# The first network's blocks 5 to 8 in pairs by seven half-block products, with attention beside blocks 2 to 4

## The chip, the cores and the metric

The kernel runs on one core of a Trainium2 chip. The metric is device time in microseconds (us) of one execution; lower is better. A core has TensorE (PE, matrix products), VectorE (DVE), ScalarE (ACT), GpSimd (POOL) and SyncE (SP), which issues nearly all DMAs here. SBUF is the memory on the core, PSUM the eight banks that TensorE writes.

## The reference, cut to what matters

Chunked attention feeds two networks of two GEMMs each; all is float32.

```python
# q, k, v: (8, 8, 576, 64); every chunk of 64 positions attends to itself only
scores = matmul(q_c, k_c.T) / sqrt(64)
attn = exp(scores - max(scores));  attn /= sum(attn) + 1e-09
x = matmul(attn, v_c)             # as 4608 tokens x 512
# first network: w_in 512 x 2048, w_out 2048 x 512
h = x @ w_in;  x = maximum(0.01 * h, h) @ w_out
# second network, the same sizes, another activation
h = x @ w_in2
P = a[0] + a[1]*h + a[2]*h**2 + a[3]*h**3
Q = 1 + abs(b[0])*abs(h) + abs(b[1])*h**2
out = (P / (Q + 1e-06)) @ w_out2
```

## The kernel before

The 4608 tokens are nine blocks of 512. A hidden layer of 2048 is 16 slices `f` of 128. To keep float32's digits, every operand of a GEMM is split into a high half that TensorE takes whole and a low half (value minus high half), and three products are added for each tile: high by high, high by low, low by high (`PASSES`). So a slice of the first GEMM is 4 x 3 = 12 products of 128x512, and so is one of the second GEMM. ScalarE makes the high half by a copy, VectorE the low half by a subtraction.

The work comes in this order:

1. The start (`start_up`): attention of the first units of 128 tokens, the decoding of the first network's weights into SBUF, where all 16 slices stay, and blocks 0 and 1 of the first network, in an order from a small planner.
2. Blocks 2 to 7 of the first network, in a loop of steps. In step `s` TensorE does `gemm1` of one slice and `gemm2` of the slice two steps earlier; ScalarE applies the leaky rectifier (`act1a`, L569) and makes the high half (`act1b`, L576), VectorE the low half (`act1c`, L581). Every four steps, one attention unit of the next block is done beside it: scores (L460), maximum and difference (L468, L470), exponential (L477), sum and reciprocal (L482 to L484), scaling on GpSimd (L488), eight transposes of pieces on VectorE (`att_turn`, L496), product with the values (L532), high and low half of the result (L547, L545). `stage_w` decodes a piece of the second network's weights and writes it to DRAM, together with the sums of quarter matrices that step 5 needs.
3. Block 8's first GEMM, all 16 slices in a row (L971); the results wait in SBUF.
4. The second network's block 0, by itself: each of 16 steps has one slice of its first GEMM and one `task`, a slice of a second GEMM (here block 8's of the first network).
5. The second network's blocks 1 to 8 as four pairs. The first GEMM of two blocks by two slices is a 2x2 by 2x2 product of half matrices, done with seven products of six matmuls each (`product`, L1060) instead of eight, from sums of weights (`wa`) and of inputs (`xf_T`). There are 32 units of two slices; a unit holds the seven products and up to four `task`s. The copies, additions and the activation around it have written times within the unit; `UNIT` is 20.43. Four banks hold the results: `a` and `b` (one tile, `hab`), `c` and `d` (`hh`). ScalarE copies the first product to `b` and, after the second, to `c`; VectorE adds the third to `a` and `d`.

The order of instructions on every engine is that in which the program issues them (`tc.manual_schedule`). In step 5 that is the order of `events`, sorted by their written times; a written time does nothing but set this order. Waits between engines come from the tiles that instructions share.

Of the kernel before, what the change touches and what calls it, by code (L numbers as in the profile page):

```python
# [17 lines left out]
P = 128  # L18
# [15 lines left out]
NSTART = 2 * NF  # L34
L1, L2 = 2, 3
# [8 lines left out]
NPAIRS = 4  # L44
# [3 lines left out]

SHIFTS = {
# [166 lines left out]
def tile_kernel(ctx: ExitStack, tc: tile.TileContext, qt, kt, vt, w1, w2, a, b, out):  # L216
# [23 lines left out]
    def singles(pool, *names):  # L240
        return [pool.tile([P, 512], F32, name=nm) for nm in names]

    hh_ps = singles(ps_open("hhp"), "hh0", "hh1")
# [6 lines left out]
    def o_acc(dc, n):  # L250
        if not o_ps:
            ps_close("startp")
            o_ps.extend(singles(ps_open("accp"), "oa0", "oa1", "ob0", "ob1"))
        return o_ps[dc][:, :n]

    xd = [dram.tile([KC, P, n], F32, name=f"xd{i}") for i, n in enumerate(BLOCKS)]
    xf = [dram.tile([4, P, 2, TM], F32, name=f"xf{j}") for j in range(NPAIRS)]
# [10 lines left out]
    wd = dram.tile([NF, P, 2, 2, DM], F32, name="wd")  # L268
    ws = dram.tile([NF // 2, P, 4, 2, 256], F32, name="ws")
    raws = {}  # L270
# [8 lines left out]
    def load_raw(ph, n):  # L279
        f, a, b = piece(ph, n)  # L280
        nm = f"raw{ph}_{n}"
        src = (w1, w2)[ph][f][:, a * DM:b * DM].bitcast(U32)
        if ph == 0 and n < NEARLY:
            raw = wpool.tile([P, (b - a) * DM, 2], U32, tag=f"w{WIDE + n % 3}", name=nm)
        else:
            raw = rpool.tile([P, DM, 2], U32, tag="raw", name=nm, bufs=3)
        nc.sync.dma_start(out=raw.rearrange("p n w -> p (n w)"), in_=src)
        raws[ph, n] = raw
# [5 lines left out]
    def temps(ph, n):  # L294
        nm = f"{ph}_{n}"
        if ph == 0 and n < NEARLY:
# [5 lines left out]
            rpool.tile([P, DM], I32, tag="dm", name=f"dm{nm}", bufs=3),  # L302
# [46 lines left out]
    def decode_lo(ph, n):  # L349
# [5 lines left out]
        if ph == 1:  # L355
            for c, y in enumerate((hi, lo)):
                nc.sync.dma_start(out=wd[f][:, c, a, :], in_=y.bitcast(F32))
# [22 lines left out]
    def form_split(f, h):  # L380
# [6 lines left out]
        for c, y in enumerate((hi, lo)):  # L387
            nc.sync.dma_start(out=ws[f // 2][:, 2 * h:2 * h + 2, c, :], in_=y.bitcast(F32))

    def stage_ops():  # L390
        for k, (f, h, _) in enumerate(halves):
            if k == 0:
                load_raw(1, 0)
            if k + 1 < NH:
                load_raw(1, k + 1)
            decode_bits(1, k)
            decode_exp(1, k)
            yield
            decode_rest(1, k)
            decode_sign(1, k)  # L400
# [15 lines left out]
    def stage_w():  # L416
        next(staging, None)
# [15 lines left out]
    def load_qk(u):  # L433
        if u >= NU:
            return
        for nm, src in (("q", qt), ("k", kt)):
            ld[nm, u] = apool.tile([P, KC, P], F32, tag=nm, name=f"{nm}{u}")
# [6 lines left out]
    def load_v(u):  # L444
        if u >= NU:
            return
        ld["v", u] = apool.tile([P, 512], F32, tag="v", name=f"v{u}")
# [16 lines left out]
    def att_max(u, ps):  # L464
        s = ps[:, :, 0:256].rearrange("p j (h t) -> p j h t", h=KC)
        mx = apool.tile([P, 8], F32, tag="mx", name=f"mx{u}")
        e = e0[u % 2] if u < NTURN else apool.tile([P, 8, CH], F32, tag="e", name=f"e{u}", bufs=1)
        V.tensor_reduce(out=mx.rearrange("p (j h) -> p j h", j=2), in_=s, axis=AX.X, op=ALU.max)  # L468
        att["e", u] = e
# [8 lines left out]

    def att_norm(u):
        e = att["e", u]  # L480
        sm = att["s", u] = apool.tile([P, 8], F32, tag="sm", name=f"sm{u}")
        V.tensor_reduce(out=sm, in_=e, axis=AX.X, op=ALU.add)  # L482
# [54 lines left out]
    def att_out(u, ps, x, off, lo):  # L537
# [8 lines left out]
        else:  # L546
            nc.scalar.activation(out=xh, in_=pv, func=AF.Copy)  # L547

# [71 lines left out]
    def finish(ph, i, share=False, cut=False):  # L620
        n = BLOCKS[i]
        for dc in range(KC):
# [8 lines left out]
            if ph == 0 and 0 < i < NB - 2 and (i % 2 or dc > 1):  # L631
                later.append((i, dc))

    later, held = [], []

    def split_later():
        if held:
            split_out(*held.pop())

    def reload_later():  # L640
        if later:
            i, dc = later.pop(0)
            held.append((i, dc, reload(i, dc)))
# [9 lines left out]
    def reload(i, dc):  # L653
        y = ypool.tile([P, TM], F32, tag="y", name=f"yr{i}_{dc}")
        nc.sync.dma_start(out=y, in_=xd[i][dc])
        return y

    x2 = {}

    def load_x2(i):  # L660
        x = new_x(1, i)
        for kc in range(KC):
            x2[kc] = ypool.tile([P, TM], F32, tag="y", name=f"x2_{i}_{kc}")[:, :BLOCKS[i]]
            nc.sync.dma_start(out=x2[kc], in_=xd[i][kc])

    def split_x2(i, kc):
        y, x = x2.pop(kc), xt[1, i]
        nc.scalar.activation(out=x[:, 0, kc, :], in_=y, func=AF.Copy)
        nc.vector.tensor_tensor(out=x[:, 1, kc, :], in0=y, in1=x[:, 0, kc, :].bitcast(F32), op=ALU.subtract)
# [13 lines left out]


    def start_up():
# [48 lines left out]
        def fin(s):  # L734
# [6 lines left out]
            "qk": load_qk, "v": load_v, "S": lambda u: att_scores(u, at_bk(u)), "mx": lambda u: att_max(u, at_bk(u)),  # L741
# [10 lines left out]
        for key, n in ordered(start_ops()):  # L752
            run[key](n)

    TAGX = [f"w{k}" for k in (0, 1, 2, 3, 4, 5, 6, 11, 15)]
    TAGB, TAGA, TAGO = ("w7", "w10"), ("w8", "w12"), ("w9", "w13", "w14")
    FORMS = ("B11", "T2", "T3", "T4", "B21", "T1", "B22")
    BASE = {"B11": 0, "B21": 1, "B22": 2}
    SUMS = {"T1": 0, "T2": 1, "T3": 2, "T4": 3}
    HALF = NF // 2  # L760
    NU2 = NPAIRS * HALF

    def second(npool, at_new):
        S, G = nc.scalar, nc.gpsimd
# [4 lines left out]
        def blocks_of(j):  # L769
            return 1 + 2 * j, 2 + 2 * j  # L770

        def sums_load(j, q, t):
            kc, c = q // 2, slice(q % 2 * 256, q % 2 * 256 + 256)
            i0, i1 = blocks_of(j)
            for x, (i, k) in enumerate(((i0, kc), (i1, kc), (i0, kc + 2), (i1, kc + 2))):
                nc.sync.dma_start(out=t[:, x], in_=xd[i][k][:, c])

        FORMED = ((3, 3, 1, "subtract"), (1, 1, 0, "subtract"), (0, 3, 0, "add"), (2, 2, 0, "subtract"))

        def sums_make(j, q, t, eng, step):  # L780
            kc, c = q // 2, slice(q % 2 * 256, q % 2 * 256 + 256)
            x, a, b, op = FORMED[step]
            eng.tensor_tensor(out=t[:, x], in0=t[:, a], in1=t[:, b], op=getattr(ALU, op))
            if step == 3:
                for x, nm in ((1, "T1"), (0, "T2"), (3, "T3"), (2, "T4")):
                    nc.sync.dma_start(out=xf[j][SUMS[nm]][:, kc, c], in_=t[:, x])

        xform = {}

        def x_load(j, n):  # L790
            nm, q = FORMS[n], len(FORMS) * j + n
            t = wpool.tile([P, 2, 2, TM], F32R, tag=TAGX[q % len(TAGX)], name=f"xf{j}_{nm}")
            xform[j, nm] = t
            if nm in SUMS:
                nc.sync.dma_start(out=t[:, 1].bitcast(F32), in_=xf[j][SUMS[nm]])
            else:
                nc.sync.dma_start(out=t.bitcast(F32), in_=xs[j][BASE[nm]])

        def x_hi(j, n):
            t = xform[j, FORMS[n]]  # L800
            S.activation(out=t[:, 0], in_=t[:, 1].bitcast(F32), func=AF.Copy)

        def x_lo(j, n, eng=V):
            t = xform[j, FORMS[n]]
# [563 lines left out]
```

## Time and profile before

| | |
|---|---|
| median of 3 runs | 1622.99 us (1622.93 to 1623.69) |
| profiled execution, whole | 1622.95 us |
| its span, first to last instruction | 1620.7 us |
| PE busy | 1603.5 us, 99% |
| DVE busy | 1211.5 us, 75% |
| ACT busy | 908.8 us, 56% |
| POOL busy | 264.3 us, 16% |
| moved by DMA | 309.85 MB, mean 191 GB/s |

Busy times are from one profiled execution. Products are pipelined and their ends are modelled: six in a row show 1.52 us where the next six begin 1.36 us later, and a wait inside a group of products shows as a longer group, not as idle time. PE's share is thus an upper limit of what it really does.

### The profile page before, as it was taken

What the parts mean: (1) busy time and instruction counts of PE and PEld (TensorE: products, weight loads), DVE (VectorE), ACT (ScalarE), POOL (GpSimd) and SP (SyncE); (2) the same over time, 40 slices, a digit from 0 to 9 for tenths busy, and PEclk for the clock granted to TensorE, in tenths of its full rate; (3) what the DMA queues carried; (4) which work ended last, traced back from release to release, by engine and by line L of the source; (5) the groups of instructions that cost most, each with busy time, mean ns of one, the idle gap of its engine ahead of it and who ended that gap; (6) DMA issues with size and microseconds to landing.
All of it is one profiled execution on the core that took longest, in us unless ns stands there. A gap on an engine that the chain in (4) does not pass through costs nothing.

```text
span 1620.7 us, 24054 instructions
## 1 busy us (share of the span) xinstructions
PE 1603.5 (99%) x9199; PEld 1317.1 (81%) x9199; DVE 1211.5 (75%) x1665; ACT 908.8 (56%) x1292; POOL 264.3 (16%) x163
## 2 busy tenths in 40 slices
PE   8999999999999999999999999999999999999998
PEld 7888788888878888888887778788888888888877
DVE  7986567666575766665257789899999999998972
ACT  7754233333433334343267777787778777777751
POOL 0000000000000000000012234333433343322210
PEclk9999999999999999999999999999999999999999
DMA  8621236343544346262466478777887778765545
GB/s 293 220 99 66 60 127 192 124 140 128 188 141 147 124 150 188 93 195 66 161 223 214 147 243 271 258 283 262 301 293 286 240 264 275 285 221 193 178 133 178
DMA packets 152401, 309.85 MB, mean 191 GB/s; under 512 B 13536, under 2 KB 46560, under 8 KB 145504
## 3 DMA queue, kind: packets, MB, share of 16 engines
q1 hardware_dynamic: 151856, 307.68, 56.8%
q8 instruction: 72, 1.18, 0.3%
q10 hardware_dynamic: 432, 0.66, 0.1%
q14 instruction: 41, 0.34, 0.1%
HBM read 242.22 MB, written 66.06 MB: 190 GB/s over the span
## 4 chain that ended last, share of the span: by engine, by line
PE 87%; DVE 6%; ACT 4%; issue 1%; DMA 1%; SPq 0%; ACTq 0%; DVEq 0%
PE hh L560 24%; PE oa L594 11%; PE ob L594 10%; PE ob L903 10%; PE oa L903 10%; PE hab L1063 10%; PE hh L1063 7%; PE hab L903 1%; PE hh L903 1%; PE at L460 1%; PE at L532 1%; ACT us L941 1%; DVE us L963 1%; DVE us L960 1%; DVE u L960 1%
## 5 line engine op out<-in xcount | busy, mean ns | idle before, releaser
L560 PE MATMUL hh<-x,w 128*128 128x512 f32 x1920 | 459.9, 390 | 0.1
L560 PEld LDWEIGHTS hh<-x,w 128*128 128x128 f32 x1920 | 359.9, 188 | 75.3 <-DVE x L545 0.5
L569 ACT ACTIVATE t<-hh 128x512 f32<-128x512 f32 x128 | 76.4, 597 | 286.2 <-PE hh L560 268.2
L947 POOL TENSOR_TENSOR u<-u,ah 128x1024 f32<-128x1024 f32 x64 | 154.3, 2413 | 275.1 <-ACT u L1102 262.0
L594 PE MATMUL oa<-g,w 128*128 128x512 f32 x768 | 198.8, 394 | 0.0
L594 PE MATMUL ob<-g,w 128*128 128x512 f32 x768 | 194.8, 389 | 0.0
L581 DVE TENSOR_TENSOR g<-t,g 128x512 fp32r<-128x512 f32 x128 | 90.5, 707 | 123.9 <-ACT g L576 119.5
L903 PE MATMUL oa<-gh,wo 128*128 128x512 f32 x512 | 178.8, 389 | 0.1
L903 PE MATMUL ob<-gh,wo 128*128 128x512 f32 x512 | 178.4, 389 | 0.0
L594 PEld LDWEIGHTS ob<-g,w 128*128 128x128 f32 x768 | 144.2, 188 | 30.2
L594 PEld LDWEIGHTS oa<-g,w 128*128 128x128 f32 x768 | 141.9, 188 | 30.2
L488 POOL TENSOR_TENSOR e<-e,sm 128x512 f32<-128x512 f32 x23 | 25.6, 1113 | 710.5 <-DVE sm L484 640.6
L903 PEld LDWEIGHTS oa<-gh,wo 128*128 128x128 f32 x512 | 96.1, 188 | 20.4 <-DVE y L923 0.5
L903 PEld LDWEIGHTS ob<-gh,wo 128*128 128x128 f32 x512 | 96.1, 188 | 20.1
L903 PE MATMUL oa<-gl,wo 128*128 128x512 f32 x256 | 99.9, 390 | 0.6 <-DVE gl L887 0.6
L1063 PE MATMUL hab<-xf_B,wb 128*128 128x512 f32 x384 | 97.7, 390 | 2.3 <-DVE gn L953 1.2
L496 DVE STREAM_TRANSPOSE pt<-e 32x256 f32<-32x256 f32 x224 | 97.5, 435 | 3.2
L903 PE MATMUL ob<-gl,wo 128*128 128x512 f32 x256 | 99.6, 389 | 0.0
L1063 PE MATMUL hh<-xf_T,wa 128*128 128x512 f32 x384 | 97.4, 389 | 0.0
L960 DVE SCALAR_TENSOR_TENSOR u<-u,ah 128x1024 f32<-128x1024 f32 x64 | 78.2, 1222 | 23.5 <-ACT ah L1113 23.4
L1063 PEld LDWEIGHTS hab<-xf_B,wb 128*128 128x128 f32 x384 | 71.8, 188 | 18.3 <-DVE sb L953 1.7
L576 ACT ACTIVATE g<-t 128x512 fp32r<-128x512 f32 x128 | 80.6, 630 | 6.7 <-PE ob L594 3.8
(194 smaller groups left out, 2652.1 us busy)
## 6 DMA issues: line engine op xcount, KB each, us to landing
wo<-wd SPq DMA_DIRECT2D x144, 512.0 KB, 5.6
wa<-ws SPq DMA_DIRECT2D x32, 1024.0 KB, 7.7
raw<-in_w SPq DMA_DIRECT2D x46, 512.0 KB, 5.1
wb<-wd SPq DMA_DIRECT2D x32, 512.0 KB, 4.4
xf_B<-xs SPq DMA_DIRECT2D x12, 1024.0 KB, 6.8
q<-in_q SPq DMA_DIRECT2D x36, 256.0 KB, 4.0
raw<-in_w SPq DMA_DIRECT2D x9, 1024.0 KB, 4.9
v<-in_v SPq DMA_DIRECT2D x36, 256.0 KB, 4.2
```

The source lines that it names most:

```text
L460: nc.tensor.matmul(ps[t, j, hp * CH:hp * CH + CH], q[r, hp, t], k[r, hp, t], start=True, stop=True)
L488: eng.tensor_tensor(out=e, in0=e, in1=sm.rearrange("p (h o) -> p h o", o=1).to_broadcast([P, 8, CH]), op=ALU.mult)
L496: nc.vector.transpose(pt[c + b:c + b + 32, :, a:a + 32], e[c + a:c + a + 32, :, b:b + 32])
L560: nc.tensor.matmul(ps, w[wp][:, 0, kc * P:(kc + 1) * P], x[:, xp, kc, :], start=(kc == 0 and (wp, xp) == (0, 0)), stop=(kc == KC - 1 and ( ...
L569: nc.scalar.activation(out=t, in_=ps, func=AF.Prelu, alpha=0.01)
L576: nc.scalar.activation(out=gh, in_=t, func=AF.Copy)
L581: nc.vector.tensor_tensor(out=gl, in0=t, in1=gh.bitcast(F32), op=ALU.subtract)
L594: nc.tensor.matmul(o_acc(dc, n), w[wp][:, 1, dc * P:(dc + 1) * P], g[gp], start=(first and (wp, gp) == (0, 0)), stop=(last and (wp, gp) == ...
L903: nc.tensor.matmul(acc(ph, i, dc), w[:, wp, c] if ph else wt[0, f][wp][:, 1, c], g[gp], start=(f == 0 and (wp, gp) == (0, 0)), stop=(f == ...
L947: G.tensor_tensor(out=u, in0=u, in1=ah, op=ALU.mult)
L960: V.scalar_tensor_tensor(out=u, in0=u, scalar=C1, in1=l, op0=ALU.add, op1=ALU.mult)
L1063: nc.tensor.matmul(bank, wform[:, wp, kc * P:kc * P + P], x[:, xp, kc, :], start=start and kc == 0 and (wp, xp) == PASSES[0], stop=kc == 1 ...
```

## The change

Three stages take the place of stages 2 and 3, and stages 4 and 5 are fed from them.

- `alone`: blocks 2 to 4 of the first network, 48 steps of a slice as before. All 23 attention units that the start leaves are done beside them, one every 10.95 of written time (a step has 5.45). Those of blocks 5 to 8 go to DRAM in one piece per unit (`att_store`, `xa`). A unit's exponential is taken head by head on ScalarE straight from PSUM, with the negated maximum as bias and the sum as a second output (`att_heads`), so that VectorE's difference and sum fall away. q, k and v have one buffer each. GpSimd joins both halves of the first network's weights again and forms their sums (`keep_w`, `first_sums`); they go to DRAM, as the second network's do. `stage_w` decodes 12 of 32 half slices here.
- `first_pairs`: blocks 5 to 8 as two pairs, 16 units of two slices, by the seven products. The units of the first pair have two `task`s each, those of the second four. Weights and inputs come from DRAM as one piece and are split on the core (`w_hi`, `w_lo`, `x_hi`, `x_lo`). An input form lies in SBUF as four runs of 128 columns for each half (`by_unit`). The activation is one Prelu. `stage_w` decodes the other 20 half slices, six or nine steps a unit.
- The second network's block 0: as before one slice and one `task` a step (two in the first two), now with written times too, and with splits of second weights and of the first pair's inputs between.

Every call of these stages and of the second network's pairs has a written time, to which a table `MOVED` of 840 entries adds its own, and `run_events` issues them sorted. The weights' DRAM copies are laid out anew so that a unit's are one DMA each. The start's list of operations, the second network's scheme of 32 units and the end stay.

```diff
@@ constants
-NPAIRS = 4
+NPAIRS, NPAIRS1 = 4, 2
+ALONE = range(2, len(BLOCKS) - 2 * NPAIRS1)
+CUT = 12
+STEP = 5.45
+MOVED = {
+    "t.act1b.11": -1.4, "t.act1b.21": 4.0, "t.act1b.25": 1.2, "t.act1b.26": 4.6, "t.act1b.33": 3.5, "t.act1b.41": 1.6,
...
@@ attention
+def att_heads(u, ps, half):
...
+    for h in range(4 * half, 4 * half + 4):
+        j, hp = divmod(h, KC)
+        nc.scalar.activation(
+            out=e[:, h], in_=ps[:, j, hp * CH:hp * CH + CH], func=AF.Exp, scale=1.0 / math.sqrt(D),
+            bias=mx[:, h:h + 1], accum_out=sm[:, h:h + 1],
+        )
+def att_store(u, ps):
...
+    nc.scalar.activation(out=y.rearrange("p h (c t) -> p c h t", c=2), in_=pv, func=AF.Copy)
+    nc.sync.dma_start(out=xa[u // 4][u % 4], in_=y.rearrange("p h t -> p (h t)"))
@@ the first network's weights
+def keep_w(f):
...
+    nc.gpsimd.tensor_tensor(out=v, in0=w[:, 0, 1, :], in1=w[:, 1, 1, :], op=ALU.add)
+    nc.sync.dma_start(out=wod[0][f // 2][:, f % 2], in_=v)
+def first_sums(k, step):
+    G = nc.gpsimd
...
+            G.tensor_tensor(out=v[-1], in0=w[:, 0, 0, :], in1=w[:, 1, 0, :], op=ALU.add)
...
+    G.tensor_tensor(out=s[:, 0], in0=a21, in1=a22, op=ALU.add)
+    G.tensor_tensor(out=s[:, 2], in0=a11, in1=a21, op=ALU.subtract)
+    G.tensor_tensor(out=s[:, 1], in0=s[:, 0], in1=a11, op=ALU.subtract)
+    G.tensor_tensor(out=s[:, 3], in0=a12, in1=s[:, 1], op=ALU.subtract)
+    nc.sync.dma_start(out=ws[0][k], in_=s)
@@ events
+def at(t, fn, *args):
+    key = f"{part_now[0]}.{fn.__name__.replace('<lambda>', 'f')}"
+    n = named[key] = named.get(key, -1) + 1
+    count[0] += 1
+    t += MOVED.get(f"{key}.{n}", 0) + 1e-6 * count[0]
+    events.append((t, len(events), fn, args))
@@ products
+def product(wform, x, bank, start, by_unit):
+    if by_unit:
+        x = x.rearrange("p c k (u t) -> p c (k u) t", u=2)
+    for kc in range(2):
+        for wp, xp in PASSES:
+            nc.tensor.matmul(
+                bank, wform[:, wp, kc * P:kc * P + P], x[:, xp, :, kc * P:kc * P + P] if by_unit else x[:, xp, kc, :],
...
+def attend(m):
+    n, t = UNITS[m], AT0 + EVERY * m
+    into_x = n // 4 < ALONE.stop
+    at(t, lambda: att_scores(n, at2))
+    if m + 1 < len(UNITS):
+        at(t + 0.8, load_qk, UNITS[m + 1])
...
+    at(t + 4.3, att_scale, n)
+    for x in range(8):
+        at(t + 5.6 + 0.9 * x, att_turn, n, x // 4, (x % 4,))
+    at(t + 15.0, lambda: att_values(n, at2))
@@ first_pairs, one unit
+        P11, PS2, PS3, P22, P12, PS1, PS4 = PT = (
+            (0.0, 2.72, 1.36, 6.8, 8.16, 9.52, 13.6), (0.0, 4.09, 8.17, 9.53, 10.9, 12.26, 16.34)
+        )[full]
+        for x in ((4.08, 10.88), (1.36, 5.45, 13.62, 17.7))[full]:
+            at(t + x, task)
...
+        at(t + P11 + 1.45, copy, b, a)
+        at(t + PS2 + 1.42, copy, c, a)
+        at(t + PS3 + 1.4, keep)
+        at(t + P12 + 1.4, add, a, a)
+        at(t + PS1 + 1.4, add, d, c)
+        at(t + P12 + 2.2, leaky, 0)
+        at(t + PS1 + 2.2, leaky, 1, 1)
+        at(t + PS4 + 1.4, leaky, 1, 0)
...
+        t += UNIT if full else 14.96
@@ the second network's block 0, one step
+        todo = [(one_block, s)] + [(one_act, s, x) for x in range(5)]
...
+            if s and x == 0:
+                todo += [(finish_one, s - 1, y) for y in range(3)]
+            todo.append((task,))
...
+        for n, call in enumerate(todo):
+            at(STEP * (s - NF + n / len(todo)), *call)
```

## Rows read from the trace of the kernel before

**Rows 1.** The page: busy time, share of the span and instructions of each engine.

```profile
PE 1603.5 (99%) x9199; PEld 1317.1 (81%) x9199; DVE 1211.5 (75%) x1665; ACT 908.8 (56%) x1292; POOL 264.3 (16%) x163
```

**Rows 2.** TensorE's waits: who for whom, us in total, times, longest.

```profile
PE hab L1063 <- DVE sb L953: 1.1, 1, 1.1
...
PE at L532 <- DVE pt L496: 1.1, 1, 1.1
...
PE hab L1063 <- ACT hab L1176: 0.7, 1, 0.7
```

**Rows 3.** Stretches: their length, busy time of each engine, granted clock, DMA share, GB/s.

```profile
200.00:300.00 100.00, 100.00 (x706) 82.00 (x703) 69.41 (x138) 35.74 (x61) 4.59 (x4) 1.00 0.47 148
...
822.00:866.00 44.00, 43.87 (x192) 35.50 (x192) 30.64 (x43) 30.25 (x47) 9.23 (x8) 1.00 0.59 207
...
913.00:1076.00 163.00, 159.26 (x694) 129.14 (x693) 144.10 (x139) 125.87 (x150) 59.76 (x35) 1.00 0.76 259
1076.00:1240.00 164.00, 164.00 (x725) 135.79 (x724) 152.84 (x139) 126.13 (x149) 59.44 (x34) 1.00 0.83 284
```

**Rows 4.** Timeline of TensorE, start and length: the start, and block 8's products.

```profile
10.55 1.06 PE L504 MATMUL hh<-ident,ep 128*128 128x128 f32 x8
...
783.06 40.96 PE L560 MATMUL hh<-x,w 128*128 128x512 f32 x180
```

**Rows 5.** The chain that ended last, block 2: start, length, what.

```profile
221.27 1.59 PE oa L594 x6
...
244.35 1.59 PE oa L594 x6
```

**Rows 6.** The same chain, in the second network's block 0.

```profile
847.59 0.82 ACT us L941
...
849.10 0.70 DVE sa L950
...
850.49 0.44 DVE g L855
...
851.09 0.70 DVE us L960
...
853.39 0.82 ACT us L941
```

**Rows 7.** Timeline of VectorE and GpSimd in the second network's pairs.

```profile
1088.14 2.39 POOL L947 TENSOR_TENSOR u<-u,ah 128x1024 f32<-128x1024 f32 x1 [0.85 <-ACT u L1102]
1088.39 3.23 DVE L887 TENSOR_TENSOR gl<-sb,gh 128x1024 fp32r<-128x1024 f32 x1
...
1102.45 1.22 DVE L887 TENSOR_TENSOR gl<-sb,gh 128x1024 fp32r<-128x1024 f32 x1
...
1105.61 2.41 POOL L947 TENSOR_TENSOR u<-u,ah 128x1024 f32<-128x1024 f32 x1 [15.08 <-ACT u L1102]
1106.23 0.68 DVE L950 TENSOR_TENSOR sb<-sb,hh 128x512 f32<-128x512 f32 x1
```

**Rows 8.** Groups of instructions by line: count, busy us, mean ns of one, idle before.

```profile
L496 DVE STREAM_TRANSPOSE pt<-e 32x256 f32<-32x256 f32 x224 | 97.5, 435 | 3.2
...
L581 DVE TENSOR_TENSOR g<-t,g 128x512 fp32r<-128x512 f32 x128 | 90.5, 707 | 123.9 <-ACT g L576 119.5 <-PE oa L594 3.7
...
L569 ACT ACTIVATE t<-hh 128x512 f32<-128x512 f32 x128 | 76.4, 597 | 286.2 <-PE hh L560 268.2 <-DVE g L581 8.2 <-DVE raw L378 7.3
...
L1183 DVE TENSOR_TENSOR hab<-hab,p 128x512 f32<-128x512 f32 x32 | 22.2, 695 | 6.2 <-PE hab L1063 6.2
...
L947 POOL TENSOR_TENSOR us<-us,tmp 128x512 f32<-128x512 f32 x16 | 20.8, 1299 | 155.4 <-ACT us L941 155.4
...
L547 ACT ACTIVATE x<-at 128x512 fp32r<-128x512 f32 x33 | 19.7, 598 | 58.1 <-DVE e L470 55.3 <-PE at L522 1.5 <-PE at L460 1.2
...
L699 ACT ACTIVATE ep<-ep,sm 128x64 f32<-128x64 f32 x64 | 16.1, 335 | 1.9 <-DVE sm L484 1.9
...
L805 DVE TENSOR_TENSOR xf_T<-xf_T 128x1024 fp32r<-128x1024 f32 x10 | 12.1, 1214 | 0.0
```

More of the change, by code (lines that the diff above doesn't have):

```diff
@@ L490, in att_scale, with att_turn @@
         )
-    def att_turn(u, half):
+    def att_turn(u, half, parts=range(4)):
         e, c = att["e", u], half * CH
-        for n in range(4):
+        for n in parts:
             a, b = n // 2 * 32, n % 2 * 32
@@ new lines, in tile_kernel @@
+    tasks, ready = [(0, ALONE[-1], NF - 2), (0, ALONE[-1], NF - 1)], {}
+    for j in range(NPAIRS1):
+        for i in blocks_of(0, j):
+            tasks.extend((0, i, f) for f in range(NF))
+    N1 = len(tasks)
+    for f in range(NF):
+        tasks.append((1, 0, f))
+    for j in range(NPAIRS):
+        for i in blocks_of(1, j):
+            tasks.extend((1, i, f) for f in range(NF))
+    late = len(tasks) - NF
+    tasks[late - 2:late + 4] = tasks[late:late + 4] + tasks[late - 2:late]
+    halved, done = [2], [0]
@@ new lines, in split_lo1, with task @@
+    def split_lo1(n):
+        t = tasks[n]
+        g, sub = ready.pop(t)
+        gh, gl = gt[t]
+        V.tensor_tensor(out=gl, in0=g, in1=gh.bitcast(F32), op=ALU.subtract)
+        left_of[sub] -= 1
+        if not left_of[sub] and sub in make:
+            free.append(sub)
+    def task(last=False):
+        ph, i, f = t = tasks[done[0]]
+        n = done[0]
+        done[0] += 1
+        g = gt.pop(t)[:2]
+        q = n // 2
+        for dc in range(KC):
+            for wp, gp in PASSES:
+                c = slice(dc * P, dc * P + P)
+                nc.tensor.matmul(
+                    acc(ph, i, dc), wo[q][:, wp, n % 2, c] if q else wt[0, f][wp][:, 1, c], g[gp],
+                    start=(f == 0 and (wp, gp) == (0, 0)), stop=(f == NF - 1 and (wp, gp) == PASSES[-1]),
+                )
+            if last:
+                put_last(dc)
+        if n % 2:
+            load_o(q + 3)
@@ new lines, in multiply, with copy @@
+    def multiply(ph, u, wname, nm, bank, start):
+        if wname[0] == "S":
+            w = wa[ph, u][:, :, int(wname[1]) - 1]
+        else:
+            c = {"A11": 0, "A12": 256, "A22": 512}[wname]
+            w = wb[ph, u][:, :, c:c + 256]
+        product(w, xform[ph, u // HALF, nm], bank, start, not ph)
+    def copy(to, of):
+        S.activation(out=to, in_=of, func=AF.Copy)
+    back = {}
+    UNITS = [13, 14, 15, *range(20, 25), *range(16, 20), *range(25, 36)]
+    UNITS = [n for n in UNITS if n < 4 * NB]
@@ L1051, in second @@
-        sb = xpool.tile([P, 4, 2, TM], F32, tag="x", name="sb")
-        for k in range(4):
-            make["sb", k] = lambda k=k: sb[:, k]
-            free.append(("sb", k))
-        make["n", 2] = lambda: ntile(2, "gn2")
-        free.append(("n", 2))
-        live = {}
-        ab, (d, c) = at_new, hh_ps[:2]
-        def product(wform, x, bank, start):
-            for kc in range(2):
+        for sub in (("w", 0), ("w", 1)):
+            if sub in free:
+                free.remove(sub)
+            del make[sub]
@@ new lines, in second, with finish_one, pre @@
+        for k in range(3):
+            make["n", k] = lambda k=k: ntile(k, f"gn{k}")
+            free.append(("n", k))
+        tmp, us = ntile(8, "tmp"), ntile(9, "us")
+        chain = {}
+        S.activation(out=warm, in_=cst[:, 0:1], func=AF.Abs_reciprocal_sqrt)
+        def finish_one(s, step):
+            u, t = chain[s]
+            (act_l, act_r, act_g)[step](*(u, tmp[:, 1], t)[:3 if step == 2 else 2])
+        def pre(n):
+            split_hi1()
+            split_lo1(n)
+        plan = {s: [(x_load, 1, 0, s)] for s in range(6)}
```

893 lines of the change are left out of this document (514 added, 379 removed), and 162 rows, old and new, of the table MOVED.

## The prediction

> **What bounds the kernel now.** I began with the page's busy row: TensorE is busy 1603.5 of 1620.7 us [rows 1]. The profiled execution took 1622.95 us, 2.25 more than its span and within 0.05 of the median of the runs, so the sum below is made against 1622.95. Next came the table of waits [rows 2]: TensorE's named waits are single events of about a microsecond. The stretches [rows 3] then say where the other engines stand. While the first network runs VectorE has 69 of 100 us; in the pairs of the second network it has 152.8 of 164 and the DMA engines 0.83, and yet TensorE is never idle there. So VectorE at 93% and 284 GB/s can be carried by this kernel without a loss, and what TensorE no longer has to do comes off the end, wherever the other engines keep up. The granted clock is 1.00 in every stretch, so the price of a product is one number: 180 in a row took 40.96 us, of which the last one's modelled tail is 0.16, so 0.2267 us each and 2.72 us for twelve [rows 4].
>
> Two places hide time that the idle column doesn't show. One attention unit costs TensorE 1.32 us: four steps with one unit are 244.35 - 221.27 = 23.08 us, and four steps alone are 4 x 5.44 = 21.76 [rows 5]. And where the second network's first block runs alone, a step takes 853.39 - 847.59 = 5.80 us instead of 5.44 [rows 6]: one round goes ScalarE 1.51, first products on VectorE, the split of the next half (850.49 to 851.09, 0.60), three more on VectorE, back to ScalarE, which writes a buffer that the last of them still read. About ten steps ran at this pace: some 3.7 us lost while PE counts as busy.
>
> **The change, part by part.** *Products.* Four blocks of the first network took 4 x 16 x 12 = 768 products in their first GEMM. Two pairs by seven half-block products take 2 x 8 x 7 x 6 = 672. The 96 that go are 96 x 0.2267 = 21.76 us; one dummy product more gives 0.23 back. The second GEMM, attention and the start keep their counts. A pair's unit with two tasks is (42 + 24) x 0.2267 = 14.96 us, one with four 20.40.
>
> The moving operand of the new products is read in four runs of 128 elements with gaps (`by_unit`). No product of the kernel before does so. Below, the cost is nothing: ScalarE reads four such runs in 598 ns and one of 512 in 597 [rows 8]. Above, each run costs like a product of 128 columns: eight took 1.06 us [rows 4], so 4 x 0.133 - 0.227 = 0.30 us times 672, or 204 us. I take nothing, since the ScalarE row is the same access pattern and the upper row also loads weights each time.
>
> *Attention beside blocks 2 to 4.* Its 23 units x 1.32 us of TensorE are moved, not removed; a unit now comes every two steps, 12.2 us. The stage is 48 x 5.44 + 23 x 1.32 = 292 us. VectorE's share of it: 48 low halves at 0.71 make 34, 184 turns at 0.435 make 80 [rows 8], maxima, sums and outputs some 37 (an estimate, 0.7 for each 512), twelve staged halves at about 5.1 (six instructions of 512 and a quarter of the sums, each 0.7 as an estimate from L581) 61, eleven low halves of 1024 at 1.21 13, so 225 of 292, 77%. ScalarE's eight exponentials by head cost 8 x 0.335 = 2.7 us a unit against one of 0.6 now: 48 us more in 292 where it has 36 in 100 [rows 3, 8], and the low half isn't needed for some two steps, so I price them at nothing. If that cover went, 2.1 us a unit would be 48 us. q, k and v keep one buffer each: the next unit's load waits at the head of SP's queue for the scores, and staging's loads and stores behind it; it is due 0.8 us after the scores and then has 11 us to land, so nothing for this either.
>
> GpSimd gets new work here: 32 additions of 512 at 1.30 [rows 8], 48 of 256 at half of that and the 23 scalings at the same 1.30, some 103 us. At 1088.39 a VectorE subtraction with two SBUF inputs took 3.23 us, having begun 0.25 us into a GpSimd multiplication of 2.39; the same one takes 1.22 with GpSimd idle [rows 7]. So an overlap costs VectorE up to the rest of the GpSimd instruction, 0.5 us on average here. GpSimd works in 35% of the stage, and some 150 VectorE instructions have two SBUF inputs: 150 x 0.35 x 0.5 = 26 us, which makes 251 of 292, still 86%. What is queued behind is the low half, two steps early, and the turns, for which the values product waits; such a wait happened once before, 1.1 us [rows 2]. I take 1 us for the stage; its bounds are 0 and 23 x 0.5 = 11.
> The Trainium skill (SBUF — State Buffer, "Who interferes with whom") says that a VectorE instruction with two SBUF inputs and a GpSimd instruction that reads SBUF exclude each other for the whole instruction. The 3.23 us agree; taken to its end, this rule is the second rival below.
>
> *The pairs.* Bank use follows the second network's scheme. The tight place is the copy of the first product's bank: ScalarE has one 1.36 us product in which to do a 0.58 us copy, and where ScalarE was late there before, TensorE waited 0.7 [rows 2]. Eight short units make 0 to 5 us. VectorE per short unit: two additions 1.4, two splits 1.4, three low halves of 1024 3.5, staging at most 5.3, so 11.6 of 14.96; per long unit at most 17.5 of 20.4. ScalarE has about 10.2 of 14.96. All are under the 93% and 77% that cost nothing [rows 3]. A short unit moves 0.52 (second weights), 0.79 and 0.52 (first weights and sums), 1.37 (staging), 0.46 (inputs), 0.65 MB (sums, outputs): 4.3 MB or 288 GB/s, just above the 284 of [rows 3]. I take 2 us for the pairs; bounds 0 and 16.
>
> *The second network's first block.* Its 16 steps and 18 tasks are 34 x 2.72 = 92.5 us. On VectorE stand 16 x 3.6, 18 splits at 0.69, twelve low halves of 1024 at 1.21 (six are new, of the second GEMM's weights, and two more of inputs), copies 2.8, one double split 1.9: 89 us, 96%. In its favour the split is written ahead of the round or behind it in many steps, which takes 0.60 off the 5.80. Against it, an addition of 1.21 fits the 1.51 us in which VectorE waits for ScalarE, but not together with the split: 5.20 + 1.21 + 0.69 - 1.51 = 5.59 in twelve steps is 1.8 us lost, and 6.4 where it fits nowhere is 11.7. I take 4, against 3.7 now: +0.3.
>
> *Entry to the second network's pairs.* The window shows 163 - 159.26 = 3.7 us idle [rows 3], partly waits for sums and banks [rows 2] that follow a burst of splits and additions; the sums are now made well before and the first product is issued early, but low halves are pushed into these units. I take 2: -1.7. The end is unchanged.
>
> Sum: 1622.95 - 21.76 + 0.23 + 1 + 2 + 0.3 - 1.7 = **1603 us**.
>
> **Rivals.**
> 1. *The pairs are bound by transfers or banks.* For it: 288 GB/s is the most this kernel would have carried for so long, and each low half stands behind a load. Against: 284 left TensorE no idle time. At the 259 GB/s of the window before it [rows 3] a short unit takes 16.6 us: 8 x 1.64 = 13 us, or 1603 - 2 + 13 = 1614. 12%.
> 2. *GpSimd holds VectorE in the attention stage; slower.* If all 103 us of GpSimd hold it, VectorE needs 225 + 103 = 328 us in a stage of 292: +36, 1603 - 1 + 36 = 1638. It decides from about 86 us held (292 - 225 + 19). For it, [rows 7]; against, half of VectorE's instructions there have one SBUF input, and one with a PSUM input took 0.68 beside GpSimd's 2.41. Half as much gives waits for turns, 1610. 12%, of which 3% for slower.
> 3. *The gaps slow the products.* Slower from 21.5 / 672 = 32 ns each. 3%.
> 4. *Better than the sum.* The first block's loss and the entry's go entirely: 1603 - 6 - 3 = 1594. 11%.
> My forecast, 1597 to 1608, has the rest, 62%.
>
> **Numbers.** The range takes in the forecast, the milder part of the second rival and about half of the first and the fourth, some 8 in 10: 1595 to 1613. Two runs of this kernel differ by 0.05%, so 0.2% (3.2 us) is about what can be told from no change. Slower than that: 3 + 3 = 6%; within it, 2%, from the tails of the first two rivals; faster, 92%.
>
> **What would show it.** 96 fewer products and 1580 to 1585 us of busy PE; new products at 1.36 us per six (rival 3: more); units of 14.96 and 20.4 us; in the attention stage 12.2 us per two steps, and values that don't wait for turns (rival 2: VectorE subtractions over 1 us, and waits for `pt`); no waits for loads in the pairs (rival 1); steps of 5.44 to 5.6 in the first block. I'd be wrong if the gaps cost time, or if a late low half stops TensorE once per unit.

## The result, and the profile after

The new kernel takes **1606.78 us** in the median of five runs (1606.05 to 1609.44). Its ratio to the kernel before is **0.9902 [0.9887, 0.9916]**, so it is about 16 us faster; 1603 had been forecast, within 1595 to 1613. The profiled execution below is the slowest of the five, 1609.44 us; a second profile comes with `new_again`.

The page's busy row, which answers to [rows 1]:

```profile
PE 1589.9 (99%) x9104; PEld 1302.0 (81%) x9104; DVE 1297.7 (81%) x1709; ACT 1018.7 (63%) x1714; POOL 400.0 (25%) x277
```

There are 95 products fewer: 96 went, the dummy came. VectorE has 86 us more work, ScalarE 110, GpSimd 136. The stretches, as in [rows 3]: the attention stage (first three), the first network's pairs (next two), the second network's first block, the entry to its pairs.

```profile
200.00:300.00 100.00, 97.75 (x796) 77.26 (x789) 74.72 (x140) 41.03 (x141) 38.21 (x33) 0.98 0.55 186
300.00:400.00 100.00, 97.68 (x880) 77.32 (x869) 78.17 (x144) 48.39 (x177) 52.74 (x49) 1.00 0.67 226
400.00:525.00 125.00, 125.00 (x1118) 98.98 (x1117) 93.81 (x193) 69.97 (x222) 22.50 (x22) 1.00 0.65 216
525.00:645.00 120.00, 120.00 (x531) 99.34 (x531) 85.72 (x121) 70.77 (x106) 18.89 (x20) 1.00 0.91 302
645.00:810.00 165.00, 164.21 (x725) 135.60 (x724) 123.81 (x181) 98.83 (x151) 17.82 (x14) 1.00 0.87 291
810.00:905.00 95.00, 95.00 (x420) 78.41 (x419) 84.44 (x110) 77.34 (x117) 22.11 (x17) 1.00 0.59 206
905.00:1068.00 163.00, 162.32 (x716) 133.84 (x715) 147.24 (x142) 128.34 (x153) 62.51 (x34) 1.00 0.78 278
```

TensorE is never idle in the pairs' first 120 us at 302 GB/s, and idle for some 4.6 us in the 200 from 200 to 400, where the attention stage begins. Its timeline where the pairs begin (start, length, line, operation, count) shows the new products:

```profile
525.96 1.52 PE L1171 MATMUL at<-xf_B,wb 128*128 128x512 f32 x6
527.32 0.39 PE L1321 MATMUL at<-xf_B,wb 128*128 128x512 f32 x1
527.55 1.52 PE L1171 MATMUL hh<-xf_T,wa 128*128 128x512 f32 x6
528.91 1.52 PE L1171 MATMUL at<-xf_T,wa 128*128 128x512 f32 x6
530.27 1.52 PE L1149 MATMUL oa<-g,w 128*128 128x512 f32 x6
```

Six products with gaps in their moving operand begin 1.36 us before the next six (527.55 to 528.91), as six without do. The same view in the attention stage holds what the forecast missed. First the kernel before, then the new one:

```profile
240.38 2.88 PE L560 MATMUL hh<-x,w 128*128 128x512 f32 x12
243.19 0.69 PE L460 MATMUL at<-k,q 64*64 64x64 f32 x32
243.71 0.65 PE L532 MATMUL at<-pt,v 64*64 64x64 f32 x32
244.28 1.66 PE L594 MATMUL oa<-g,w 128*128 128x512 f32 x6
```

```profile
245.90 0.69 PE L770 MATMUL at<-pt,v 64*64 64x64 f32 x32
246.52 1.66 PE L838 MATMUL oa<-g,w 128*128 128x512 f32 x6
248.02 1.52 PE L838 MATMUL ob<-g,w 128*128 128x512 f32 x6
249.47 0.69 PE L679 MATMUL at<-k,q 64*64 64x64 f32 x32
250.09 3.02 PE L804 MATMUL hh<-x,w 128*128 128x512 f32 x12
252.95 1.52 PE L838 MATMUL oa<-g,w 128*128 128x512 f32 x6
```

Before, a unit's scores (L460) are followed at once by the values of the one ahead of it (L532). In the new kernel values (L770) and scores (L679) stand apart, with full products between them. From 248.02 six products last until 249.38; the scores start at 249.47, the next group at 250.09, and that group's twelve products last 2.86 where twelve take 2.72. So the scores alone cost 0.09 + 0.62 + 0.14 = 0.85 us; with the values a unit costs some 1.7 this way, not the 1.32 of [rows 5].

**The ledger of the stage.** I take the attention stage from the first full product after 217.6 us to the pairs' first product, 218.24 to 525.96 here: 307.7 us, where the work as forecast (48 x 5.44 + 23 x 1.32) is 291.5. A group of full products should last 0.2267 us each, 32 small ones 0.65. What a group lasts beyond that is called lost, where it is over 0.25 us. The lost time adds up to 8.3 us; the rest, 299.4, is 7.9 more than the work as forecast. In this profile and in that of `early_no_sums`, 1.7 us of the lost time are products at the lower of TensorE's two clocks (last section). The same for all kernels below, from their profiles:

| kernel | stage | lost | rest |
|---|---|---|---|
| the new kernel | 307.7 | 8.3 | 299.4 |
| `new_again` | 305.2 | 5.3 | 299.9 |
| `first_load_early` | 304.2 | 4.5 | 299.7 |
| `no_weight_sums` | 302.3 | 2.0 | 300.3 |
| `whole_exponential` | 305.8 | 6.2 | 299.6 |
| `together_in_after` | 301.2 | 8.0 | 293.3 |
| `together_loads_too` | 302.3 | 9.2 | 293.1 |
| `all_repairs` | 302.0 | 9.1 | 292.9 |
| `all_together_early` | 307.9 | 13.2 | 294.7 |
| `early_no_sums` | 301.0 | 7.6 | 293.4 |
| `heads_half_early` | 299.5 | 6.2 | 293.3 |

By the same reckoning the first network's pairs lost 1.1 us, the second network's first block 0.2 (before: 3.7), its pairs and the end 3.4 (before: 6.9).

### The profile page after: what moved, and what is told of

Read it like the earlier page. It is cut to its first block, busy times and chain, and to the rows that moved or that the text cites. A ratio compares the mean times of both kernels' runs of the same rounds, so it can differ in the third digit from the quotient of the medians.

```text
span 1607.7 us, 24575 instructions
## 1 busy us (share of the span) xinstructions
PE 1589.9 (99%) x9104; PEld 1302.0 (81%) x9104; DVE 1297.7 (81%) x1709; ACT 1018.7 (63%) x1714; POOL 400.0 (25%) x277
## 3 DMA queue, kind: packets, MB, share of 16 engines
q8 instruction: 72, 1.18, 0.3%
## 4 chain that ended last, share of the span: by engine, by line
PE 92%; DVE 5%; ACT 1%; DMA 1%; issue 0%; POOL 0%; SPq 0%; ACTq 0%; DVEq 0%
PE at L1171 16%; PE oa L1149 16%; PE ob L1149 16%; PE hh L1171 12%; PE hh L804 12%; PE oa L838 6%; PE ob L838 6%; PE hh L1512 3%; PE at L1149 1%; PE hh L1149 1%; PE at L679 1%; PE at L770 1%; DMA k<-in_k 1%; DVE pt L734 1%; ACT e L710 1%; DVE g L825 1%
## 5 line engine op out<-in xcount | busy, mean ns | idle before, releaser
L804 PE MATMUL hh<-x,w 128*128 128x512 f32 x960 | 233.8, 394 | 0.2 <-DVE x L783 0.2
L804 PEld LDWEIGHTS hh<-x,w 128*128 128x128 f32 x960 | 177.3, 188 | 38.6 <-DVE x L783 0.5
L1022 POOL TENSOR_TENSOR st<-st 128x256 f32<-128x256 f32 x96 | 93.3, 972 | 285.9 <-DMA st<-xd 152.1
L1171 PE MATMUL at<-xf_B,wb 128*128 128x512 f32 x576 | 146.3, 389 | 0.6 <-DVE sb L1461 0.6
L1171 PEld LDWEIGHTS hh<-xf_T,wa 128*128 128x128 f32 x576 | 108.0, 188 | 23.5 <-DVE gn L1461 1.1
L1171 PEld LDWEIGHTS at<-xf_B,wb 128*128 128x128 f32 x576 | 108.0, 188 | 23.4 <-DVE sb L1461 1.0
L838 PE MATMUL oa<-g,w 128*128 128x512 f32 x468 | 122.6, 397 | 0.3 <-DVE yq L861 0.3
L838 PE MATMUL ob<-g,w 128*128 128x512 f32 x468 | 119.8, 392 | 0.0
L838 PEld LDWEIGHTS oa<-g,w 128*128 128x128 f32 x468 | 86.3, 188 | 19.3 <-DVE yq L861 0.7
L1149 PE MATMUL ob<-g,wo 128*128 128x512 f32 x384 | 97.5, 389 | 0.0
```

The source lines that it names most:

```text
L804: nc.tensor.matmul(ps, w[wp][:, 0, kc * P:(kc + 1) * P], x[:, xp, kc, :], start=(kc == 0 and (wp, xp) == (0, 0)), stop=(kc == KC - 1 and ( ...
L838: nc.tensor.matmul(o_acc(dc, n), w[wp][:, 1, dc * P:(dc + 1) * P], g[gp], start=(first and (wp, gp) == (0, 0)), stop=(last and (wp, gp) == ...
L1149: nc.tensor.matmul(acc(ph, i, dc), wo[q][:, wp, n % 2, c] if q else wt[0, f][wp][:, 1, c], g[gp], start=(f == 0 and (wp, gp) == (0, 0)), s ...
L1171: nc.tensor.matmul(bank, wform[:, wp, kc * P:kc * P + P], x[:, xp, :, kc * P:kc * P + P] if by_unit else x[:, xp, kc, :], start=start and ...
```

## The experiments

**Theory 1:** most of the miss is that a unit's scores and values no longer stand together on TensorE. **Theory 2:** it is waits in the attention stage, from GpSimd holding VectorE or from ScalarE's heads. Two smaller questions: the first load of k, and where the first block's gain came from.

**`apart_in_before`**: scores ahead of the first GEMM, values behind it.

```diff
-                ps = gemm1(0, i, f)
-                if f == 0:
-                    new_x(0, i + 1)
                 if r == 0 and n < NU:
                     load_v(n)
                     att_scores(n, at2)
+                ps = gemm1(0, i, f)
+                if f == 0:
+                    new_x(0, i + 1)
                 if r == 0:
                     att_values(u, at2)
```

> The kernel before, with the scores of a unit written ahead of the first GEMM of their step and the values left behind it, so that the two groups of 64x64 products no longer stand back to back on TensorE. Theory 1 (a group of small products that stands alone between full products costs TensorE 0.86 us, two back to back 1.32): 23 units x 0.40 = 9.2 us more, 1632. Theory 2 (the attention stage of the new kernel loses its time to GpSimd and ScalarE, which hold back VectorE): nothing changes, 1623 within 1.

1632.43 us against 1623.61, ratio 1.0052 [1.0037, 1.0067]: 8.8 us more, 0.38 a unit. TensorE's timeline:

```profile
217.86 0.69 PE L460 MATMUL at<-k,q 64*64 64x64 f32 x32
218.48 3.02 PE L560 MATMUL hh<-x,w 128*128 128x512 f32 x12
221.43 0.69 PE L532 MATMUL at<-pt,v 64*64 64x64 f32 x32
222.06 1.66 PE L594 MATMUL oa<-g,w 128*128 128x512 f32 x6
```

No wait came with it; the stage's only lost time is one of 1.29 us, for turns, as before [rows 2]. Theory 1 holds in a kernel that has none of the new stage.

**`together_in_after`**: a unit's scores take the place right behind the values that precede them; 20 of 23 do.

```diff
+            if getattr(fn, "kind", None) == "values":
+                last = t
+            if getattr(fn, "kind", None) == "scores" and last is not None and t - last < TOGETHER:
+                events[n] = last + 1e-9, n, fn, args
...
+    TOGETHER = 7.5
```

> The new kernel, with the scores of a unit moved up behind the values that precede them wherever a product group stood between (20 of the 23 units in the first network). Theory 1: 20 x 0.40 = 8.0 us less, 1599 against 1606.8, and one unit's two groups take 1.32 us together. Theory 2: nothing gained, 1606 to 1608, since the waits for turns and exponentials stay; scores that come earlier could even wait more.

1603.61 us, 0.9877 [0.9862, 0.9891]. The stage's rest fell by 6.1 to 6.6 us, 0.31 to 0.33 for each unit put together, but lost time rose from 5.3 to 8.0: in the stage k now came late five times, 4.0 us in all, where it had come late once (1.1 to 1.7). So the mechanism is right and 3 to 4 us of the 8 were gained at once; the remainder turned into waits, mostly for loads.

**`no_weight_sums`**:

```diff
-        nc.gpsimd.tensor_tensor(out=v, in0=w[:, 0, 1, :], in1=w[:, 1, 1, :], op=ALU.add)
+        nc.gpsimd.memset(v, 0.0)
...
-        G.tensor_tensor(out=s[:, 0], in0=a21, in1=a22, op=ALU.add)
+        for x in range(4):
+            G.memset(s[:, x], 0.0)
```

> The new kernel, with GpSimd writing zeros in place of the weight sums of the first network (its 32 additions of 512 and 48 of 256 are left out, so those products multiply zeros). A write of zeros reads nothing from SBUF. Theory 2: VectorE's subtractions go back from 0.81 to 0.71 us, the waits in the attention stage (some 4 us) go, 1602 to 1604. Theory 1: those waits are not GpSimd's in the main; 0 to 2 us less, 1605 to 1607.

1603.63 us, 0.9876 [0.9861, 0.9890]. Groups by line, VectorE's low halves, first in the new kernel (218 to 526 us), then here (218 to 526 us): count, busy, mean ns.

```profile
L825 DVE TENSOR_TENSOR g<-t,g 128x512 fp32r<-128x512 f32 x49 | 43.5, 887 | 18.1 <-ACT g L820 17.4
```

```profile
L823 DVE TENSOR_TENSOR g<-t,g 128x512 fp32r<-128x512 f32 x49 | 34.7, 707 | 19.2 <-ACT g L818 18.5
```

The subtraction is back at the 707 ns of [rows 8], and of the stage's lost 5.3 us only the first load's 2.0 is left. These are TensorE's waits in the stage in `new_again` (three rows), and here:

```profile
PE at L679 <- DVE x L783: 1.2, 2, 1.0
PE at L679 <- DMA k<-in_k: 1.1, 1, 1.1
PE at L770 <- ACT e L710: 1.1, 2, 0.7
```

```profile
PE at L677 <- DMA k<-in_k: 1.7, 1, 1.7
```

The waits that go are those of scores for VectorE's low half of a result (L783) and of values for ScalarE's exponentials (L710), which stand behind VectorE's maxima. A rival would be that GpSimd, with less to do, came earlier to its scalings (L726); but what VectorE's turns waited for the scalings hardly changed (11.2 us in the new kernel, 10.7 here), and in neither profile does TensorE wait for turns by name. So GpSimd's hold is real and costs TensorE 3 to 4 us (theory 2 as far as GpSimd goes); the rest of the ledger, 300.3, didn't move. VectorE is busy 215.6 us of the stage here and 234.1 with the sums: their hold takes 18.5. GpSimd's writes of zeros, 64 of them (32 of 512 and 32 of 256 elements, not the 48 that I had expected; 16 sums of inputs and the 23 scalings go on), hold nothing: by the rule of the Trainium skill (SBUF — State Buffer, "Who interferes with whom") a GpSimd instruction that only writes SBUF doesn't contend with a VectorE instruction with two SBUF inputs, and the 707 ns agree.

**`whole_exponential`**:

```diff
-            V.tensor_scalar(out=mx, in0=mx, scalar1=-1.0 / math.sqrt(D), scalar2=None, op0=ALU.mult)
-            att["m", u] = mx
-            return
+            e = apool.tile([P, 8, CH], F32, tag="e", name=f"e{u}", bufs=2)
...
+            att_exp(u)
...
+        V.tensor_reduce(out=sm, in_=e, axis=AX.X, op=ALU.add)
```

> The new kernel with the exponential of a unit as before: VectorE subtracts the maxima, ScalarE takes one exponential of 512, VectorE adds up. ScalarE gets back eight exponentials and eight reads of the accumulator (4.1 us a unit for 0.6), VectorE gets 1.4 us a unit more. Theory 1: TensorE is not bound by either in the attention stage, 1607 within 1.5. Theory 2 with ScalarE as the one that is late: 2 to 4 us less, 1603 to 1605. If VectorE is what is late: 2 to 10 us more, the 23 x 1.4 = 32 us on VectorE showing as waits for turns.

1608.24 us, 0.9908 [0.9892, 0.9925]: not to be told from the new kernel. ScalarE is busy 113.7 us of the stage and not 154.5, VectorE 257.7 and not 234.1, and TensorE has neither gained nor lost: waits for exponentials (some 1 us) went, and those for VectorE's low half of the result rose from 1.2 to 3.3 us. So the heads are at most a small part of what the stage loses; as the change gives VectorE what it takes from ScalarE, this run can't say more. The 4.1 us a unit in this expectation, and in a later one, was my misreading: the records of two kinds of instruction that it adds up overlap in time.

**`split_before_round`**:

```diff
+            pre(2)
             act_abs(ps, tmp[:, 0], u)
...
-            pre(2)
```

> The kernel before, with one statement moved: where the second network's first block runs, the split of the next half step stands ahead of the round's first products and not in the middle of it. If the middle split is what makes a step 5.80 us, steps fall to 5.44 and the ten of them give 3.7 us back: 1619.5 to 1620. If the new kernel gained its 3.5 us there by something else (another order of the low halves, data there earlier), nothing changes: 1623 within 1.

1618.94 us, 0.9967 [0.9954, 0.9979], 5.6 us less than the kernel before beside it (1624.54). The chain that ended last, at the place of [rows 6]:

```profile
848.42 2.72 PE hh L560 x12
851.14 1.36 PE oa L903 x6
852.50 1.36 PE ob L903 x6
853.86 2.72 PE hh L560 x12
```

VectorE and ScalarE are gone from it, a step is 853.86 - 848.42 = 5.44, and the block loses nothing. In the profile 3.7 us are gained in the block and 1.3 at the entry to the pairs behind it (lost 4.7 before, 3.4 here). So the split's place is the cause, and part of the entry's loss hangs on it too.

**`first_load_early`** moves the first load of the stage, and puts the load of partial sums that followed it (`get_part`) 3.4 of written time later; **`together_loads_too`** is `together_in_after` with the loads moved up, **`all_repairs`** is both.

```diff
+        for nm, src in (("q", qt), ("k", kt)):
+            ld[nm, NSTARTED] = ypool.tile([P, KC, P], F32, tag="y", name=f"{nm}first")
+            nc.sync.dma_start(out=ld[nm, NSTARTED], in_=src[NSTARTED].rearrange("p (h t) -> p h t", h=KC))
...
-        at(2.8, get_part)
+        at(6.2, get_part)
```

```diff
+                x = next(x for x, e in enumerate(events) if e[2] is load_qk and e[3] == (UNITS[fn.unit + 1],))
+                events[x] = min(events[x][0], last + 0.1), *events[x][1:]
```

> The new kernel, with q and k of the first unit of the attention stage loaded at the end of the start, into two tiles of their own. If that load is late because it is issued late: the wait of 1.66 us and the 0.3 beside it go, 2.0 us less, 1604.8, and the granted clock stays 1.00 behind it. If the wait only hides that TensorE would wait for the next unit anyway: 1606.8 within 0.7.

> The new kernel, with the scores of 20 units moved up behind the values, and now the load of the next unit's q and k moved up with them. If k was late in together_in_after because its load stood at its old place behind other transfers: the 3.2 us of waits for k behind the first go, 1600 to 1601. If k is late because it has only one buffer and a transfer takes 4 us or more beside the weights: the waits stay, 1603.6 within 0.7.

> The new kernel with the repairs of together_loads_too and first_load_early at once. Theory 1 with late loads as the rest: 2.0 us under together_loads_too, 1598 to 1599. If GpSimd's hold on VectorE is what then ends last: the waits come back as waits for turns and exponentials, 1602 to 1604.

They took 1606.26 (0.9890 [0.9876, 0.9903]), 1604.08 (0.9879 [0.9864, 0.9894]) and 1601.70 us (0.9864 [0.9851, 0.9878]). The early load takes the wait at 221 us away, but its 2.0 us didn't come. What the first two runs changed is within what their intervals can tell: the early load's gain by the ledger is 0.8 to 1.0 us (stage 304.2 for 305.2). With the loads moved up, waits for k fell from 4.0 to 2.0 us, and waits of values for exponentials rose from 2.1 to 4.3: nothing gained, so late loads were not the last thing to end. `all_repairs` kept those waits (4.2 us) as well, and came 2.4 us below `together_loads_too`, some 3 to 4 above the 1598 to 1599 of its first theory. Its profile, of the slowest of its four runs, has one more wait, of 2.5 us: TensorE waited for VectorE's copy of a finished block's output (L1164), and VectorE stood behind a staging step of ScalarE that waited for a DMA. In `together_loads_too` the same wait is 0.2 us.

**`new_again`**, the new kernel once more; **`all_together_early`**, which also moves a unit's maximum and exponentials up with its scores (by 6.9 us of written time); **`early_no_sums`**, the same without GpSimd's sums.

```diff
+                for x, e in enumerate(events):
+                    if getattr(e[2], "unit", None) == fn.unit or e[2] is load_qk and e[3] == nxt:
+                        events[x] = e[0] - early, *e[1:]
```

> The new kernel once more, unchanged, beside the two below on one chip, and for a second profile of it. Every theory: 1606 to 1608. If the fall of the granted clock at 224 to 228 us belongs to the wait for k at 221, this profile shows it again; if it only happened in one execution, the wait of 1.7 us stands here without it.

> As all_repairs, and the maximum and the exponentials of a unit moved up with its scores (all_repairs left them at their old place, and values waited five times, 4.2 us, for the exponential that stood just before them). If that place is what costs: those waits go, 3 to 4 us less than all_repairs, 1598 to 1599. If GpSimd's hold on VectorE is what ends last: the waits come back in another place, 1601 to 1602.

> As all_together_early, with GpSimd writing zeros in place of the weight sums of the first network (these products multiply zeros; the additions are left out). It is the floor that theory 1 gives without GpSimd's hold: no waits over 0.5 us in the attention stage, some 293 to 294 us for the stage against 307.7 in the new kernel, 1595 to 1597. If it is no faster than all_together_early, GpSimd's hold has stopped to cost anything once the order is right.

1607.07 us (0.9897 [0.9884, 0.9911]), 1609.66 (0.9918 [0.9904, 0.9931]) and 1602.61 (0.9868 [0.9855, 0.9882]). The second was a miss by over 10 us, and the third missed the floor by 6; it is 7 us faster than the second, so GpSimd's sums cost in this order too. VectorE's timeline in `all_together_early`, and then TensorE's:

```profile
389.14 1.33 DVE L734 STREAM_TRANSPOSE pt<-e 32x256 f32<-32x256 f32 x3
394.13 0.69 DVE L783 TENSOR_TENSOR x<-at,x 128x512 fp32r<-128x512 f32 x1 [3.66 <-ACT e L710]
394.73 0.88 DVE L734 STREAM_TRANSPOSE pt<-e 32x256 f32<-32x256 f32 x2
395.62 0.69 DVE L825 TENSOR_TENSOR g<-t,g 128x512 fp32r<-128x512 f32 x1
```

```profile
392.92 0.39 PE L838 MATMUL oa<-g,w 128*128 128x512 f32 x1
396.37 1.43 PE L838 MATMUL oa<-g,w 128*128 128x512 f32 x5 [3.06 <-DVE g L825]
```

The step's low half (L825) stands on VectorE behind the low half of a result (L783), and that waited 3.66 us; the row names ScalarE's exponentials, the last of which ended at 394.1. TensorE waited 3.06 us for the step's low half. The same 3.06 us wait stands in `early_no_sums` too, so the sums aren't its cause. Here ScalarE's heads do cost time, because of where they stand.

**`heads_half_early`**: as `all_repairs`, maximum and exponentials 3.0 us earlier.

```diff
-                        events[x] = e[0] - early, *e[1:]
+                        events[x] = e[0] - min(early, 3.0), *e[1:]
```

> As all_repairs, with the maximum and the exponentials of a unit moved up by 3.0 us of written time and not by the full 6.9 (moved in full, they put 4.1 us of ScalarE and a maximum in front of the steps' own halves, and one wait alone was 3.06 us). If the place behind the scores is what decides: the five waits of values for exponentials (4.2 us) go and no 3 us wait comes, 1598 to 1600. If VectorE and ScalarE have no room for these beside GpSimd's hold wherever they stand: 1601 to 1604.

**1599.48 us** (1598.28 to 1601.78), 0.9848 [0.9834, 0.9861], which is below both kernels. Four of the five waits for exponentials went (1.2 us is left of 4.2); 2.8 us of waits for k are left, and one of 0.9 for turns. TensorE's timeline, to hold against the one of the new kernel above:

```profile
254.06 1.52 PE L838 MATMUL ob<-g,w 128*128 128x512 f32 x6
255.51 0.69 PE L770 MATMUL at<-pt,v 64*64 64x64 f32 x32
256.03 0.65 PE L679 MATMUL at<-k,q 64*64 64x64 f32 x32
256.60 5.74 PE L804 MATMUL hh<-x,w 128*128 128x512 f32 x24
```

Between the end of the full products (254.06 + 1.36 = 255.42) and the next stand 1.18 us for two groups; with the 0.14 behind them that is the 1.32 of [rows 5] again. Against `all_repairs` the two intervals overlap, and not all between the two profiles is the heads': 3.0 us of waits for exponentials and the 2.5 for L1164's copy went, 2.6 for k and 0.4 for turns came. Against the new kernel (1606.7 to 1607.6 in `new_again`) the runs don't overlap, and the gain is 7.6 us.

## Why the prediction was right, and where it was not

The time lies in the range and the sign is right, but the sum comes so near by terms that cancel, which is luck. TensorE's busy time shows it: 1589.9 us, where 1580 to 1585 was to be seen. Against the second profile of the new kernel (`new_again`, that execution 1607.60 us):

- **Products.** Right: 95 fewer, 0.2267 us each. So was the gap term at nothing: six at 1.36 us. That rules out rival 3.
- **Attention stage.** The step that failed is "Its 23 units x 1.32 us of TensorE are moved, not removed". The 1.32 was read from [rows 5], where scores and values stand back to back ([rows 5] is a chain over four steps and doesn't show their order; the timeline above does), and carried into a stage in which the diff writes scores at `t` and values at `t + 15.0`. Apart, a unit costs some 1.7: 299.9 - 291.5 = 8.4 us more, 0.37 a unit, shown from both sides by `apart_in_before` and `together_in_after`. Its waits, taken as 1 with bounds 0 and 11, are 5.3: the first load of k 1.4, which had been costed at nothing ("has 11 us to land"; the first unit has none), and 3 to 4 that go with GpSimd's sums. Together the stage is 305.2 where 292.5 was forecast, +12.7.
- **GpSimd's hold.** Sized at 26 us of VectorE; the weight sums alone measure 18.5, the 23 scalings and 16 sums of inputs were not taken out. VectorE is busy 234 of 308 us where 251 of 292 was forecast. The second rival's milder form was thus right in kind: 3 to 4 us on TensorE, not the 8 that it gave, and as waits for L783 and L710, not for turns.
- **ScalarE's heads.** Sized at 2.7 us a unit, right in size: ScalarE's busy time differs by 154.5 - 113.7 = 40.8 us, 1.8 for each of 23 units, which with the 0.63 of one whole exponential makes 2.4. The cover held, as costed, but for some 1 us of waits for exponentials, which went with GpSimd's sums; `all_together_early` shows what it takes to lose it.
- **The first network's pairs.** 1.1 us lost where 2 was taken: -0.9. Rival 1 is ruled out, 302 GB/s without a wait for a load.
- **The second network's first block.** Forecast +0.3, measured -3.5. I took the new low halves to cost more than the split's new place gives back. VectorE, sized at 89 of 92.5 us, is busy 84.4 of 95, which leaves room for both. With the entry below this is rival 4. `split_before_round` shows in the kernel before that the split's place alone takes the 5.80 us step to 5.44; in the new kernel's own order I did not vary it.
- **Entry to the second network's pairs.** Forecast -1.7, measured -3.5 over these pairs and the end: the entry alone lost 4.7 before and 0.8 now, one wait. `split_before_round` gains 1.3 of it in the kernel before; the cause of the remainder is open.

Besides, one wait of 1.3 us for turns in the stage before [rows 2] has no counterpart in the new ledger, and the stage begins some 0.5 us later (218.56; 218.0 in the profile of `no_weight_sums`). In this execution the granted clock was 0.51 from 24.5 to 28 us, in the start, and in that of `no_weight_sums` it wasn't. 1603.0 + 12.7 - 0.9 - 3.8 - 1.8 - 1.3 + 0.5 = 1608.4, against 1607.6. So the forecast was some 4 us low because 12.7 us of one stage were missed and nearly 8 elsewhere were left out on the other side.

**Open:** which of VectorE's instructions, under the hold, makes the low half L783 and the maxima late for which TensorE waits; and whether another order takes the 6 us that `heads_half_early` still loses. Theory 1 explains the rest of the ledger, 2 the lost time in part; with scores and values together, waits take other places in every order that I ran.

## What to carry to other kernels

A price read where two small groups of products stand back to back holds only there: before such a price is moved, look at what will stand on either side of it on TensorE. Where an order is written out by hand, the gain of a better order on one engine comes back as waits on the next; move the followers of a moved instruction by what their own engines have free, not by the same amount (here 3.0 of written time took 10 us less than the full 6.9). And a chain of a few engines that sets a step's length is worth looking through for a piece that isn't part of the recurrence: one statement moved gave the kernel before 5 us.

## What the runs showed of the hardware

**Small products cost at their borders.** 32 products of 64x64 between full ones cost 0.85 us, 64 in one piece 1.32, so the second change from full products to small ones and back costs 0.38; by whole runs 8.8 / 23 = 0.38 (`apart_in_before`).

**A sum as second output of ScalarE is a second instruction.** Groups by line in the attention stage of the new kernel:

```profile
L710 ACT ACTIVATE e<-at,mx 128x64 f32<-128x64 f32 x184 | 55.1, 325 | 40.8 <-DVE mx L690 40.8
L710 ACT ACTIVATION_READ_ACCUMULATOR e<-at,mx 128x1 f32 x184 | 39.9, 217 | 0.0
```

The records overlap: their sum is 95.0 us for 23 units, 4.1 each, while ScalarE is busy with a unit's heads for 2.4 (worked out above from `whole_exponential`).

**The granted clock fell behind two waits, and not behind others as long.** Stretches from 219 to 228 us of the new kernel's first profile, then of its second:

```profile
219.00:221.00 2.00, 2.00 (x10) 1.50 (x8) 0.78 (x2) 0.04 (x1) 0.76 (x1) 1.00 0.46 130
221.00:223.00 2.00, 0.34 (x6) 0.10 (x6) 0.40 (x1) 1.23 (x2) 0.00 (x0) 1.00 0.82 279
...
224.00:228.00 4.00, 4.00 (x12) 3.11 (x11) 0.55 (x2) 2.48 (x16) 0.00 (x0) 0.57 1.01 338
```

```profile
219.00:221.00 2.00, 2.00 (x11) 1.63 (x10) 0.79 (x2) 0.37 (x2) 1.08 (x1) 1.00 0.60 175
221.00:223.00 2.00, 0.86 (x20) 0.47 (x22) 0.10 (x1) 1.23 (x2) 0.00 (x0) 1.00 0.84 247
...
224.00:228.00 4.00, 4.00 (x19) 3.29 (x18) 0.36 (x2) 2.48 (x16) 0.00 (x0) 1.00 0.78 274
```

After the first network's blocks at full clock TensorE stood still for 1.66 us, waiting for k. In the first profile the clock then was at 0.50, the lower of its two levels (1.2 GHz), for some 3 us, and two groups of six products took 2.04 and 2.41 us in place of 1.36: 1.7 us lost. The second profile, with a wait of 1.14, and `no_weight_sums`, with 1.72, stayed at 1.00. It fell a second time in `early_no_sums`, behind the wait of 3.06 us:

```profile
388.40 2.20 PE L836 MATMUL oa<-g,w 128*128 128x512 f32 x5 [3.06 <-DVE g L823]
390.40 2.38 PE L836 MATMUL ob<-g,w 128*128 128x512 f32 x6
```

The mean granted clock from 388.5 to 392 us is 0.54 there, and five and six products took 2.00 and 2.21 us: again 1.7 us lost. `all_together_early`, with the same wait of 3.06 us, stayed at 1.00 behind it. So the wait alone doesn't decide it, and what does is open.
